# Second-layer tails of a 512-token tile in one row-tiled group over all PSUM banks, with output projections one chunk behind

## The chip, the cores and the metric

The kernel runs on one core of one Trainium2 chip. The metric is the device time of one execution in microseconds (us), as a median over runs. Before the change it is 214.68 us (6 runs, 214.44 to 214.84).

## The reference, cut to what matters

Two branches read the same 2048 x 640 input and a gate mixes them per token. Branch A is a diagonal complex state-space recurrence with an input and an output projection. Branch B is a two-layer perceptron with 1728 hidden features.

```python
x = A_x                                                   # 1 x 2048 x 640
g = sigmoid((x * gate_w).sum(-1, keepdims=True))
# branch A
Bu = einsum("bld,pd->blp", x, B_bar)                      # complex, P = 640
h_t = Lam_bar * h_{t-1} + Bu_t                            # for each token t
a = 2 * einsum("blp,dp->bld", hseq, C).real + x * Dskip
# branch B, F = 1728 = 13 * 128 + 64
hid = gelu(einsum("bsd,df->bsf", x, w1) + b1)
b = einsum("bsf,fd->bsd", hid, w2) + b2
return g * a + (1 - g) * b
```

The 1728 hidden features are 13 full blocks of 128 and a tail of 64. The tail is what the change is about.

## The kernel before

**Tiles.** The 2048 tokens are worked in 4 tiles of 512 (index `q`), in 8 recurrence blocks of 256 (index `b`), and in 16 output chunks of 128 (index `c`, four to a tile). All matmul results go to the 8 PSUM banks, handed out in a ring by `next_bank()`.

**Stages of one tile.**
- `bproj(q)`: input projection of the recurrence, L680, 10 banks of five matmuls. ScalarE moves each bank to `U` (L689).
- `ssm(b)`: VectorE only. Four multiplies and adds ("pre"), two scans (L720) with small carry steps, four multiplies and adds ("post") that write `H[b % 3]`.
- `m1(q)`: first perceptron layer, L640, 13 banks of five matmuls. ScalarE applies the gelu and writes `Gl[q % 2]` (L647).
- `m1_tail(q)`: the 64 tail features of two tiles at once, L658, in one bank. Four gelus on 64 partitions each (L667) write them twice, to partitions 0 to 63 and 64 to 127 of `Gl`.
- `gates(q)`: VectorE row sums, a tanh on ScalarE (L604), and two small VectorE steps that write the gate columns `gcol` and `g1col` (L608, L609).
- `outs(...)`: second layer, output projection and mixing for some chunks.

**Inside `outs`.** For each chunk:
- `m2_prime(c)`: ScalarE writes the bias into the chunk's two banks, one for each half of 320 output columns (L754). The matmuls then add to it.
- `m2_main(c)`: 13 matmuls for each half, 26 in all (L767).
- `m2_tails(cs)`: the 64 tail features for all chunks of the call (L781). The left half uses partitions 0 to 63 and the right half 64 to 127, so two matmuls lie on two row tiles of the array. The group follows the first chunk's main product, so it needs the primed banks of every chunk of the call.
- `m2_out(c)`: ScalarE scales the two banks by `g1col` into `E1[c % 3]` (L795).
- `cproj(c)`: output projection of the recurrence, 10 matmuls for each half (L815), in two further banks. ScalarE scales these by `gcol` into `E2[c % 3]` (L826).
- `comb(c)`: VectorE computes the skip term `xg` (L834), adds `xg`, `E1` and `E2` in two steps (L481, `osb`), and SyncE stores 160 KB (L868). The last chunk adds `xg` and `E1` first, then finishes straight out of PSUM in two column parts of 384 and 256 (L848) with two stores (L854).

**What sets the order.** Each stage registers operations with an engine, an assumed duration, what they read and write, and a priority. A list scheduler (`Sched.order`) then fixes one static order for each engine. An operation of TensorE takes its priority from the order of registration. Each engine runs its list strictly in that order and waits on semaphores for what it needs. `op(..., writes)` makes a writer of a buffer wait for all its earlier readers, so a bank, an `E1` copy or an `H` block is written only after its last use.

## Time and profile before

| quantity | value |
|---|---|
| median of 6 runs | 214.68 us |
| profiled execution, device time | 214.44 us |
| profiled execution, span from first to last instruction | 213.1 us |
| granted TensorE clock | 1.0 of full speed |
| main products, L767 | 416 matmuls, 59.1 us busy |
| tails, L781 | 32 matmuls, 3.4 us busy |
| output projections, L815 | 320 matmuls, 46.1 us busy |
| primes, L754 | 32, 0.441 us each |
| first evictions, L795 | 32, 0.526 us each |
| scans, L720 | 16, 2.812 us each |

The span leaves out 1.34 us of the device time that lies around the instructions. Matmuls are pipelined, so the busy time of a group is not a sum that adds up to the span; the chain of waits in order of time is what shows how long TensorE takes for a stage. Lines of `kernel.py` are written as L and a number. A duration belongs to one profiled execution, and the median of runs is 0.24 us above it.

### The profile page before, as it was taken

How to read it: one execution, taken by the hardware profiler on the slowest of the kernel's cores; microseconds unless marked ns; L12 is line 12 of the kernel's file. 1: busy time of each engine (PE TensorE's matmuls, PEld its weight loads, DVE VectorE, ACT ScalarE, POOL GpSimd, SP SyncE). 2: the span in 40 equal slices, each digit the busy share in tenths (PEclk: the TensorE clock that was granted, in tenths of full speed). 3: DMA queues.
4: the chain of work that ended last, by engine and by line, in shares of the span. 5: the costliest groups of instructions: out<-in, count | busy, mean ns of one | idle time of the engine just before them, and what ended most of it. 6: DMA issues, size and time to landing. Idle time of an engine off the chain costs nothing.

```text
span 213.1 us, 3104 instructions
## 1 busy us (share of the span) xinstructions
PE 209.5 (98%) x1254; PEld 119.8 (56%) x1264; DVE 188.7 (89%) x262; ACT 113.2 (53%) x205; POOL 2.5 (1%) x10
## 2 busy tenths in 40 slices
PE   8999999999999999999999999999999999999996
PEld 3444444444567675444467767444446777677673
DVE  2599999999899999999999959999999998988712
ACT  2489556679444234557835332556786454535230
POOL 1000000000000000000000010000000000000000
PEclk9999999999999999999999999999999999999999
DMA  5999899999000040000000013000000010001000
GB/s 142 332 241 196 222 384 198 159 217 162 0 0 34 31 138 18 31 0 0 0 3 0 31 43 146 22 8 0 3 0 2 0 34 31 31 3 62 31 34 31
DMA packets 31114, 16.08 MB, mean 75 GB/s; under 512 B 22908, under 2 KB 30332, under 8 KB 31100
## 3 DMA queue, kind: packets, MB, share of 16 engines
q1 hardware_dynamic: 30752, 14.57, 28.5%
q0 software_dynamic: 288, 1.31, 1.9%
q8 instruction: 10, 0.16, 0.3%
q14 instruction: 4, 0.03, 0.0%
q10 hardware_dynamic: 60, 0.01, 0.0%
HBM read 7.63 MB, written 2.62 MB: 48 GB/s over the span
## 4 chain that ended last, share of the span: by engine, by line
PE 97%; DMA 1%; issue 0%; DVE 0%
PE ps L767 27%; PE ps L640 22%; PE ps L815 21%; PE ps L680 20%; PE ps L620 4%; DMA xn<-in_A_x_dram 1%; PE ps L781 1%; PE ps L658 1%; PE ps L412 0%; DVE osb L848 0%; PE ps L431 0%
## 5 line engine op out<-in xcount | busy, mean ns | idle before, releaser
L767 PE MATMUL ps<-W2sb,Gl 128*128 128x320 bf16 x416 | 59.1, 299 | 0.0
L767 PEld LDWEIGHTS ps<-W2sb,Gl 128*128 128x128 bf16 x416 | 40.6, 98 | 16.5 <-ACT Gl L647 0.4
L640 PE MATMUL ps<-xT,W1sb 128*128 128x512 bf16 x215 | 47.5, 379 | 0.3
L815 PE MATMUL ps<-CT,H 128*128 128x320 bf16 (+2 forms) x320 | 46.1, 299 | 0.0
L720 DVE TENSOR_TENSOR_SCAN W<-atab,V 128x1280 bf16<-128x1280 f32 x16 | 44.3, 2812 | 0.3
L680 PE MATMUL ps<-xT,BT 128*128 128x512 bf16 x196 | 43.1, 379 | 0.3 <-issue 0.2
L815 PEld LDWEIGHTS ps<-CT,H 128*128 128x128 bf16 x320 | 30.7, 98 | 13.5 <-issue 1.6
L795 ACT ACTIVATE E<-ps,g1col 128x320 bf16<-128x320 f32 x32 | 16.1, 526 | 40.5 <-PE ps L781 21.5
L640 PEld LDWEIGHTS ps<-xT,W1sb 128*128 128x128 bf16 x220 | 21.5, 98 | 26.0
L647 ACT ACTIVATE Gl<-ps,cols 128x512 bf16<-128x512 f32 x44 | 29.7, 690 | 11.6 <-PE ps L640 11.6
L680 PEld LDWEIGHTS ps<-xT,BT 128*128 128x128 bf16 x200 | 19.5, 98 | 23.4 <-ACT Gl L647 0.4
L689 ACT ACTIVATE U<-ps 128x512 bf16<-128x512 f32 x40 | 23.6, 595 | 15.7 <-PE ps L680 15.7
L826 ACT ACTIVATE E<-ps,gcol 128x320 bf16<-128x320 f32 x30 | 15.8, 527 | 18.0 <-PE ps L815 18.0
L754 ACT ACTIVATE ps<-b2b 128x320 f32<-128x320 bf16 x32 | 14.1, 441 | 1.0
L834 DVE SCALAR_TENSOR_TENSOR xg<-xn,gcol,dsk 128x640 bf16<-128x640 bf16 x16 | 13.8, 882 | 0.4
L481 DVE TENSOR_TENSOR osb<-xg,E 128x640 bf16<-128x640 bf16 x15 | 7.3, 486 | 7.7 <-ACT E L826 7.6
L597 DVE SCALAR_TENSOR_TENSOR scr<-xn,gwb 128x640 bf16<-128x640 bf16 x16 | 13.2, 823 | 0.4
L481 DVE TENSOR_TENSOR H<-H,V 128x1280 bf16<-128x1280 bf16 x16 | 12.5, 822 | 0.3
L481 DVE TENSOR_TENSOR V<-V,W 128x1280 bf16<-128x1280 bf16 x16 | 12.5, 821 | 0.3
L481 DVE TENSOR_TENSOR V<-mr,U 128x2560 bf16<-128x2560 bf16 x8 | 11.9, 1490 | 0.2
L481 DVE TENSOR_TENSOR H<-c,W 128x2560 bf16<-128x2560 bf16 x8 | 11.9, 1489 | 0.1
L481 DVE TENSOR_TENSOR V<-s,W 128x2560 bf16<-128x2560 bf16 x8 | 11.9, 1485 | 0.0
(79 smaller groups left out, 102.6 us busy)
## 6 DMA issues: line engine op xcount, KB each, us to landing
out_dram<-osb SPq DMA_DIRECT2D x15, 160.0 KB, 1.8
W2sb<-in_B_w_dram SPq DMA_DIRECT2D x1, 2080.0 KB, 11.1
xn<-in_A_x_dram POOLq DMA_DIRECT2D x2, 640.0 KB, 4.7
W1sb<-in_B_w_dram SPq DMA_DIRECT2D x4, 256.0 KB, 4.3
xn<-in_A_x_dram SPq DMA_DIRECT2D x1, 640.0 KB, 7.2
W1sb<-in_B_w_dram SPq DMA_DIRECT2D x1, 480.0 KB, 5.4
W1sb<-in_B_w_dram SPq DMA_DIRECT2D x1, 400.0 KB, 6.2
xn<-in_A_x_dram SPq DMA_DIRECT2D x1, 384.0 KB, 5.7
```

The source lines that it names most:

```text
L481: return inc("dve", nc.vector.tensor_tensor(out=o, in0=a, in1=b, op=o_))
L640: t = nc.tensor.matmul(PS[bank][:, :], W1sb[:, k, jf * 128:(jf + 1) * 128], xT[q][:, k, :], start=(k == 0), stop=(k == KD - 1))
L647: return inc("act", nc.scalar.activation(Gl[q % 2][:, jf, :], PS[bank][:, :], ACT.Gelu_apprx_tanh, bias=b1col[:, jf:jf + 1]))
L680: t = nc.tensor.matmul(PS[bank][:, :], BT[:, ci, kd, k * 128:(k + 1) * 128], xT[q][:, kd, :], start=(kd == 0), stop=(kd == KD - 1))
L689: return inc("act", nc.scalar.activation(dst, src, ACT.Copy, scale=1.0 if ci == 0 else -1.0))
L720: t = inc("dve", nc.vector.tensor_tensor_scan(out=g[:, ci, :], data0=a, data1=v[:, ci, :], initial=0.0, op0=ALU.mult, op1=ALU.add))
L754: return inc("act", nc.scalar.activation(PS[bank][:, 0:HALF], b2b[:, cols], ACT.Copy))
L767: t = nc.tensor.matmul(PS[bank][:, 0:HALF], Gl[q % 2][:, jf, t4 * 128:(t4 + 1) * 128], W2sb[:, jf, cols], start=False, stop=False, skip_gr ...
L795: return inc("act", nc.scalar.activation(E1[c % NE][:, cols], PS[bank][:, 0:HALF], ACT.Copy, scale=g1col[:, c:c + 1]))
L815: t = nc.tensor.matmul(PS[bank][:, 0:n], H[b % NHB][:, ci, k, s * 128:(s + 1) * 128], CT[:, ci, k, cols], start=(i == 0), stop=(i == 2 * K ...
L826: return inc("act", nc.scalar.activation(E2[c % NE][:, cols], PS[bank][:, 0:HALF], ACT.Copy, scale=gcol[:, c:c + 1]))
L834: return inc("dve", nc.vector.scalar_tensor_tensor(out=xg[c % 2][:, :], in0=xn[q % 2][:, c % 4, :], scalar=gcol[:, c:c + 1], in1=dsk[:, :] ...
```

## The change

Before, a call of `outs` takes two or three chunks, so a tile of four chunks has its tails in two groups (the last two tiles together in three), and a chunk's projection follows its own main product at once. After it, a call takes a whole tile: all eight banks are primed, the first main product runs, and one group of eight tail matmuls serves four chunks. Each chunk's projection and mixing are registered after the next chunk's main product; the last chunk's projection follows that of the chunk before. The recurrence block 7 (`ssm(2 * NQ - 1)`), which stood between two calls, is registered through `mid` within the third tile's call, after the projection of chunk 9. The order of all other stages in the text is as it was. The static orders of ScalarE and VectorE change with it, since the scheduler places their operations by when it expects them to be ready.

```diff
-        def outs(*cs):
+        def outs(q, mid=None):
+            cs = range(4 * q, 4 * q + 4)
             for c in cs:
                 m2_prime(c)
             for c in cs:
                 m2_main(c)
                 if c == cs[0]:
                     m2_tails(cs)
                 m2_out(c)
-                cproj(c)
-                comb(c)
+                if c > cs[0]:
+                    cproj(c - 1)
+                    comb(c - 1)
+                    if mid is not None and c == cs[0] + 2:
+                        mid()
+            cproj(cs[-1])
+            comb(cs[-1])
...
         gates(1)
-        outs(0, 1)
-        outs(2, 3)
+        outs(0)
         for q in range(2, NQ):
...
             gates(q)
             if q < NQ - 1:
-                outs(4 * q - 4, 4 * q - 3)
-                outs(4 * q - 2, 4 * q - 1)
-        outs(NCH - 8, NCH - 7, NCH - 6)
-        ssm(2 * NQ - 1)
-        outs(NCH - 5, NCH - 4, NCH - 3)
-        outs(NCH - 2, NCH - 1)
+                outs(q - 1)
+        outs(NQ - 2, mid=lambda: ssm(2 * NQ - 1))
+        outs(NQ - 1)
```

The new order on TensorE, after `bproj(1)`, reads: 26 main, 8 tails, 39 main (chunk 1 and half of chunk 2), 20 projection, 13 main, 20 projection, 26 main, 40 projection. The later tiles have 26 main, 8 tails, 26 main, 20 projection, 26 main, 20 projection, 26 main, 40 projection. The old order had 26 main, 4 (or 6) tails, 20 projection, and then 26 main and 20 projection in turn.

## The prediction

> **What bounds the kernel now.** I read the page's busy shares first, then its chain of work, then the chain in order of time around one stage, then the tail instructions alone, and last ScalarE's timeline where a prime comes latest.

> ```profile
> PE 209.5 (98%) x1254; PEld 119.8 (56%) x1264; DVE 188.7 (89%) x262; ACT 113.2 (53%) x205; POOL 2.5 (1%) x10
> PE 97%; DMA 1%; issue 0%; DVE 0%
> ```

> TensorE's matmuls fill 98% of the span and carry 97% of the chain that ends last; VectorE is at 89%, ScalarE at 53%. A busy matmul row isn't a proof of pace, so what counts is the chain in time. Its piece for the first two groups of output chunks:

> ```profile
> 56.42 3.53 PE ps L767 x26
> 59.95 0.38 PE ps L781 x4
> 60.33 2.82 PE ps L815 x20
> 63.15 3.53 PE ps L767 x26
> 66.68 2.72 PE ps L815 x20
> 69.40 3.53 PE ps L767 x26
> 72.93 0.38 PE ps L781 x4
> 73.31 2.82 PE ps L815 x20
> 76.13 3.53 PE ps L767 x26
> 79.66 2.72 PE ps L815 x20
> ...
> 182.18 0.51 PE ps L781 x6
> 182.70 2.82 PE ps L815 x20
> ```

> Columns are start, length, what. Each piece begins where the last ends: TensorE waits for nobody here. L767 is a chunk's main product (26 matmuls), L781 the tails, L815 the output projection (20). The reader is to see two things. Four tail matmuls take 0.38 us and six 0.51, so two more, one pair on the two row tiles, cost 0.13. And the projection takes 2.82 after tails but 2.72 elsewhere.

> ```profile
>   issue: 1.8, 7
>   ACT E L795: 21.5, 7
> ```

> These come from the view of line L781: before each of the 7 tail groups weight loading sat idle, 1.8 us together, 0.26 each, with nothing but issue to wait for. The second line says that ScalarE waits for the tails, not the reverse.

> [...] two pairs at 0.13 are 0.26, the group takes 0.38, so 0.12 goes on entry, and 0.10 on the way back, 0.22 per group. [...] here each tail pair needs two banks, hence all eight for four chunks. [...]

> **The change part by part.**

> *Fewer tail groups.* Before there are 7: five of 4 matmuls and two of 6, 5 x (0.38 + 0.10) + 2 x (0.51 + 0.10) = 3.62 us. After there are 4 of 8 matmuls. Eight matmuls weren't seen; by the step from four to six they take 0.51 + 0.13 = 0.64, and 4 x (0.64 + 0.10) = 2.96. Gain 0.66, all on the chain. Bounds: if the two row tiles lost their overlap in a longer group, the added pair would cost 0.26 instead of 0.13, 4 x 0.13 = 0.5 back; it can't be below 0.13, the time of one matmul of the pair (3.53 / 26 = 0.136 for the same 320 columns), so there is no further gain. I take 0.13, because four to six showed it. What follows the tails is now a main product, not a projection; it has the same shape, and 0.12 (0.11 is what it lost after the first-layer tail L658: 3.64 against 3.53) against 0.10 is nothing.

> *The same matmuls otherwise.* The new order on TensorE has the same 416 main, 32 tail and 320 projection matmuls. In the first group the half of the third main product comes ahead of the first projection; order alone costs nothing between full-array matmuls (3.53 and 2.72 follow each other without a gap).

> *Eight primes before the tails.* The group now waits for all eight banks to be written with the bias (L754, 0.44 us each) instead of four. Behind the waiting tail stands all of TensorE. Where the primes stand in ScalarE's queue, by the changed order:
> - First group: a prime follows each U eviction (L689), 0.58 + 0.44 = 1.02 per pair against the 1.08 of a bank's five matmuls (U starts at 54.30, 55.38, 56.46 in ScalarE's timeline). The last eviction starts at 56.46, so the last prime ends near 57.5; the tails start at 59.95. Slack 2.4.
> - Second: gelu and prime pairs. They keep the pace of 1.08 in the trace, see below. The last gelu starts at 107.24, the last prime ends near 108.4, the tails start at 110.73. Slack 2.3.
> - Third, the tight one: the eighth prime takes the bank of the first-layer tail (L658), so it stands behind four 64-partition gelus (L667).

> ```profile
> 156.58 0.44 ACT L754 ACTIVATE ps<-b2b 128x320 f32<-128x320 bf16 x1
> 156.96 0.67 ACT L647 ACTIVATE Gl<-ps,cols 128x512 bf16<-128x512 f32 x1
> 157.66 0.44 ACT L754 ACTIVATE ps<-b2b 128x320 f32<-128x320 bf16 x1
> 158.04 0.67 ACT L647 ACTIVATE Gl<-ps,cols 128x512 bf16<-128x512 f32 x1
> 159.23 2.81 ACT L667 ACTIVATE Gl<-ps,cols 64x512 bf16<-64x512 f32 x4 [0.52 <-PE ps L658]
> 162.75 0.58 PE L781 MATMUL ps<-W2sb,Gl 64*128 64x320 bf16 x6
> ```

> The reader is to see that gelu and prime overlap a little, so that a pair fits into 1.08, and that 0.52 of idle time after the last gelu takes a seventh prime (0.44). The four tail gelus end at 162.04, the eighth prime at 162.48, and the tails are due at 162.8: slack 0.3. Before, they needed only two of those gelus. Bounds for a stall: 0 to 0.2, [...] I take 0.
> - Fourth: primes follow projection evictions, the last one about 1.1 us after the last projection of the third group; the tails are 3.5 after it. Slack 2.4.

> *Projections one chunk behind.* Each chunk's projection uses banks that the first eviction (L795, 0.53) cleared a main product earlier, so the bank wait is looser. In the first group VectorE now runs the scan (5.54, with its small steps 6.3) before it computes the gate columns. So the first eviction can start only near 56.67 + 6.3 + 0.3 = 63.3 instead of 60.37. Its banks are wanted at the first projection, which starts after tails, one and a half main products: 60.59 + 0.10 + 3.53 + 1.77 = 66.0. Slack 2.

> *Buffers.* E1 has three copies and is now filled one main product plus one projection, 6.3 us, ahead. The eviction of chunk 7 (L795) waits for the sum of chunk 4, which in VectorE's order moved behind a scan: counted from the second group's start, that sum ends at 16.2 (pre-work ends 8.9, scan 6.3, sum 1.0) and is wanted at 18.5. If late it would hold ScalarE, then chunk 7's projection at 23.0. The H blocks are read later than before and their writers wait: block 3 (written from 106.42) needs the projection of chunk 1, over by 73.2; block 7 is placed after chunk 9's projection. The input load of tile 2 on GpSimd's queue waits for chunk 3's VectorE product, some 4 us later than 74.1; its data are first read after 132. SyncE's queue has the same stores in the same order.

> *The end.* The projection of chunk 14 now comes after the last main product, so its eviction and its sum (L481, two of 0.49) stand just before the last chunk's finishing steps. Before, that sum ended 1.61 us after chunk 14's projection and the first finishing step began 1.67 after the last projection's start. So it fits with 0.06 to spare, and the second step has another 0.47 of idle time. The 160 KB store of chunk 14 is issued about 1.6 us ahead of the last one; such stores land in 1.8. I take 0 for it; bounds below.

> **Sum.** Profiled execution: span 213.10 plus 1.34 around it = 214.44. Minus 0.66: 213.78. The median shown is 0.24 above the profiled run, so 214.68 - 0.66 = 214.0.

> **Rivals.** "Same" below is within 0.2%, 0.43 us, about what this measurement can tell from no change.
> - *Gain eaten by small waits*: the third group's 0.3 slack fails by 0.2 and the end store adds some 0.2, or longer groups pack worse (up to 0.5 back). Speaking for it: the slack is thin and a group of eight wasn't seen. Against: gelu and prime kept pace six times in a row. 0.66 - 0.4 leaves 0.26: 214.4. Chance 0.19.
> - *The end store decides, slower*: the last store queues behind chunk 14's 160 KB. If the last three stores were strictly one after another, with 1.8, 1.6 and 1.5 us, the last would land 1.8 later. It turns the gain into a loss beyond 0.2% from 0.66 + 0.43 = 1.09 on. Against: before, the last two stores overlapped by 0.65 us and each still landed in 1.6 and 1.5. At the full price: 214.0 + 1.8 = 215.8; at 1.3, which I'd expect of it, 215.3. Chance 0.11.
> - *The change doesn't do what it says*: excluded by the instruction order, which shows four groups of eight.

> **How the numbers follow.** The forecast (214.0) has 0.70. Its own range is 213.7 to 214.25: 0.3 below for the scatter of the medians (runs shown span 0.40) and up to where 0.2% ends. The second case reaches to 214.6, and the range 213.7 to 214.6 leaves out the slower case and a little of the rest. Faster 0.70, same 0.19, slower 0.11.

> **What would show it.** In the changed profile: L781 pieces of x8 at 0.64, main products of 3.63 after them, every projection of 2.72; a TensorE chain of the same unbroken form, span near 212.4. I'd be wrong if L781 is preceded by a wait for L754 (third group first), if L815 waits for L795, or if the stretch from the last matmul to the end of the span, 2.1 us before, grows.

## The result, and the profile after

The median fell from 214.64 us (42 runs, among them the 6 with 214.68 above) to 214.13 us (21 runs, 213.64 to 214.61). The ratio is 0.9975 with a 95% interval of 0.9968 to 0.9982, so between 0.39 and 0.69 us were gained. The profiled execution took 213.86 us, with a span of 212.5.

The page's busy shares and chain of work, after:

```profile
PE 208.3 (98%) x1254; PEld 119.9 (56%) x1264; DVE 189.1 (89%) x262; ACT 113.4 (53%) x205; POOL 2.5 (1%) x10
PE 95%; DMA 2%; issue 1%; ACTq 1%; POOL 0%; DVE 0%; POOLq 0%
```

TensorE still carries the chain. The 2% of DMA are a load at the very start (the bias rows, 4.51 us from 2.61 on), not a wait in the stages that changed. The chain in order of time (start, length, what), first tile and third tile:

```profile
56.47 3.53 PE ps L767 x26
60.01 0.65 PE ps L781 x8
60.66 5.40 PE ps L767 x39
66.06 2.72 PE ps L815 x20
68.78 1.77 PE ps L767 x13
70.54 2.72 PE ps L815 x20
73.26 3.53 PE ps L767 x26
76.79 5.43 PE ps L815 x40
...
158.81 3.64 PE ps L767 x26
162.45 0.65 PE ps L781 x8
163.10 3.64 PE ps L767 x26
166.74 2.72 PE ps L815 x20
...
204.99 5.45 PE ps L815 x40
```

Three things are to be seen. The pieces still join without a gap (a single record of L767 lasts 0.299 us in both profiles and 26 of them take 3.53, so records overlap and only the pieces are compared). A group of eight takes 0.65 us. And the extra 0.10 to 0.11 now falls on the main product after the tails (3.64 against 3.53; 5.40 for 39 against 1.5 x 3.53 = 5.30), while a projection of 20 takes 2.72 everywhere. The 3.64 at 158.81 stands ahead of the tails: it follows the first-layer tail (L658), as it did before the change.

The last projection of the kernel before is this piece of its chain:

```profile
208.28 2.73 PE ps L815 x20
```

From the start of the first main product to the end of the last matmul TensorE needed 208.28 + 2.73 - 56.42 = 154.59 us before and 204.99 + 5.45 - 56.47 = 153.97 after, so 0.62 less. This measure, called the *stretch* below, leaves out the start of the kernel, in which TensorE has the same work in all kernels here but which ended anywhere between 56.31 and 56.94 in their profiles. That scatter is as large as the gain, and it passes on to the whole: the two profiled runs of the changed kernel (213.86 and, in the next section, 214.21) differ by 0.35 us, and the starts of their first main products by 0.36. So the medians need many runs to show the gain.

### The profile page after: what moved, and what is told of

It is laid out like the page before. It is cut to its first block, busy times and chain, and to the rows that moved or that the text cites. A ratio compares the mean times of both kernels' runs of the same rounds, so it can differ in the third digit from the quotient of the medians.

```text
span 212.5 us, 3107 instructions
## 1 busy us (share of the span) xinstructions
PE 208.3 (98%) x1254; PEld 119.9 (56%) x1264; DVE 189.1 (89%) x262; ACT 113.4 (53%) x205; POOL 2.5 (1%) x10
## 4 chain that ended last, share of the span: by engine, by line
PE 95%; DMA 2%; issue 1%; ACTq 1%; POOL 0%; DVE 0%; POOLq 0%
PE ps L767 27%; PE ps L640 22%; PE ps L815 20%; PE ps L680 20%; PE ps L620 3%; DMA rows<-in_B_b_dram 2%; PE ps L781 1%; PE ps L658 1%; ACTq L325 1%; DVE osb L848 0%; POOL io_i L381 0%; PE ps L431 0%; POOL rows L371 0%; POOL st_i L383 0%; POOL st_i L382 0%
## 5 line engine op out<-in xcount | busy, mean ns | idle before, releaser
L767 PE MATMUL ps<-W2sb,Gl 128*128 128x320 bf16 x416 | 59.2, 299 | 0.0
L767 PEld LDWEIGHTS ps<-W2sb,Gl 128*128 128x128 bf16 x416 | 40.3, 98 | 17.2 <-issue 1.1
L815 PE MATMUL ps<-CT,H 128*128 128x320 bf16 (+2 forms) x320 | 45.4, 299 | 0.0
L815 PEld LDWEIGHTS ps<-CT,H 128*128 128x128 bf16 x320 | 31.3, 98 | 12.2
L795 ACT ACTIVATE E<-ps,g1col 128x320 bf16<-128x320 f32 x32 | 16.2, 526 | 37.8 <-PE ps L767 25.0
L640 PEld LDWEIGHTS ps<-xT,W1sb 128*128 128x128 bf16 x220 | 21.5, 98 | 26.0
L647 ACT ACTIVATE Gl<-ps,cols 128x512 bf16<-128x512 f32 x44 | 29.6, 688 | 10.4 <-PE ps L640 10.4
L689 ACT ACTIVATE U<-ps 128x512 bf16<-128x512 f32 x40 | 23.6, 595 | 14.4 <-PE ps L680 14.4
L481 DVE TENSOR_TENSOR osb<-xg,E 128x640 bf16<-128x640 bf16 x15 | 7.3, 487 | 9.2 <-ACT E L826 9.2
L754 ACT ACTIVATE ps<-b2b 128x320 f32<-128x320 bf16 x32 | 14.1, 442 | 1.1
L481 DVE TENSOR_TENSOR H<-H,V 128x1280 bf16<-128x1280 bf16 x16 | 12.5, 822 | 0.3
L481 DVE TENSOR_TENSOR V<-V,W 128x1280 bf16<-128x1280 bf16 x16 | 12.5, 821 | 0.3
L481 DVE TENSOR_TENSOR V<-mr,U 128x2560 bf16<-128x2560 bf16 x8 | 11.9, 1490 | 0.3
L481 DVE TENSOR_TENSOR H<-c,W 128x2560 bf16<-128x2560 bf16 x8 | 11.9, 1488 | 0.1
L481 DVE TENSOR_TENSOR W<-mi,U 128x2560 bf16<-128x2560 bf16 x8 | 11.9, 1485 | 0.0
```

The source lines that it names most:

```text
L481: return inc("dve", nc.vector.tensor_tensor(out=o, in0=a, in1=b, op=o_))
L640: t = nc.tensor.matmul(PS[bank][:, :], W1sb[:, k, jf * 128:(jf + 1) * 128], xT[q][:, k, :], start=(k == 0), stop=(k == KD - 1))
L647: return inc("act", nc.scalar.activation(Gl[q % 2][:, jf, :], PS[bank][:, :], ACT.Gelu_apprx_tanh, bias=b1col[:, jf:jf + 1]))
L689: return inc("act", nc.scalar.activation(dst, src, ACT.Copy, scale=1.0 if ci == 0 else -1.0))
L754: return inc("act", nc.scalar.activation(PS[bank][:, 0:HALF], b2b[:, cols], ACT.Copy))
L767: t = nc.tensor.matmul(PS[bank][:, 0:HALF], Gl[q % 2][:, jf, t4 * 128:(t4 + 1) * 128], W2sb[:, jf, cols], start=False, stop=False, skip_gr ...
```

## The experiments

Each kernel is the changed one with one edit, and "after" is the changed kernel. "Stretch" is read from its own chain in the same way.

**The changed kernel again** (no edit), for a comparison beside the next three.

> The changed kernel as it is, beside the others. Both theories: 0.9975 of before, within 0.9968 to 0.9982; some 214.1 us.

Measured: 214.11 us, ratio 0.9971 (0.9959 to 0.9982), stretch 153.96. The result repeats.

**Two groups of four for each tile.**

```diff
-                if c == cs[0]:
-                    m2_tails(cs)
+                if c % 2 == 0:
+                    m2_tails((c, c + 1))
```

> Projections one chunk behind as after, but two groups of four tails per tile, 8 groups in all. If each group costs a fixed 0.22 us for entering and leaving the row tiles: 4 groups more than after, +0.88, 215.0 us, and 0.22 above before with its 7. If the later projections bring the gain and not the number of groups: as after, 214.1 us.

Measured: 214.95 us, ratio 1.0004 (0.9995 to 1.0013), stretch 154.81, between these two pieces of its chain:

```profile
56.46 3.53 PE ps L767 x26
...
205.82 5.45 PE ps L815 x40
```

That is 0.84 more than after, or 0.21 for each of four added groups, and 0.22 more than before for one added group. The projections are one chunk behind as after, and yet nothing is left of the gain. So the number of groups makes the gain, not the place of the projections.

**One group of two for each chunk.**

```diff
-                if c == cs[0]:
-                    m2_tails(cs)
+                m2_tails((c,))
```

> As after, but each chunk has its own group of two tails, 16 groups. Fixed price per group: 12 more than after, 12 x 0.22 = +2.64, 216.8 us, with L781 pieces of x2 at 0.25 us. If the number of groups doesn't matter: 214.1 us.

Measured: 216.66 us, ratio 1.0093 (1.0079 to 1.0108), stretch 156.51: 2.54 more than after, again 0.21 for each of twelve groups. Its chain, and what stood ahead of its tails in the view of line L781:

```profile
56.39 3.53 PE ps L767 x26
...
207.10 0.24 PE ps L781 x2
207.35 5.55 PE ps L815 x40
...
  issue: 4.0, 15
```

A group of two takes 0.24 and costs 0.10 on the 40 projection matmuls behind it (5.55 against the 5.45 of the same last piece after the change). Weight loading sat idle 0.27 us ahead of each of 15 groups with nothing but issue to wait for, about as it did before. With 0.24, 0.38, 0.51 and 0.65 for two, four, six and eight tails, a pair costs 0.135 and the entry into the group 0.11.

**Projections registered at once.**

```diff
-                if c > cs[0]:
-                    cproj(c - 1)
-                    comb(c - 1)
-                    if mid is not None and c == cs[0] + 2:
-                        mid()
-            cproj(cs[-1])
-            comb(cs[-1])
+                cproj(c)
+                comb(c)
+                if mid is not None and c == cs[0] + 1:
+                    mid()
```

> Four groups of eight as after, but each projection is registered right after its own main product; the scheduler puts half a main product between where it expects a wait. If the number of groups makes the gain: as after, 214.1 us, no wait on TensorE. If being one chunk behind makes it: as before, 214.6 us.

Measured: 214.24 us, ratio 0.9974 (0.9963 to 0.9985), stretch 153.96, and no wait of TensorE in the tiles. The list scheduler put main products between the tails and the first projection by itself: one and a half in the first tile, half a one in each of the other three. First and second tile:

```profile
61.00 5.40 PE ps L767 x39
66.41 5.43 PE ps L815 x40
...
111.57 1.87 PE ps L767 x13
113.44 2.72 PE ps L815 x20
```

So being a whole chunk behind isn't needed in the last three tiles; half a main product to run while the first eviction is done is enough. The first tile, where the eviction waits for the scan, had its cover here too.

**Projections forced to be at once.** The same edit, and each main product is held until the projection before it is done, so the scheduler can't put anything between.

```diff
-                   [("bank", bank)], f_mm, prio=pe_prio())
+                   [("bank", bank)], f_mm, prio=pe_prio(), after=last_c)
...
-                op(f"c_{c}_{hf}", "pe", ...)
+                last_c[:] = [op(f"c_{c}_{hf}", "pe", ...)]
```

> Four groups of eight, and each main product is held until the projection of the chunk before is done, so the first projection of a tile follows the tails at once. If being behind covers the wait for the first eviction: in the first tile the projection waits for the gate columns after the scan, 63.3 + 0.53 - 60.7 = 3.1 us, in the other three for one eviction, 0.58 each; 4.8 in all, 218.9 us. If the order has no part in it: 214.1 us.

Measured: 221.25 us, ratio 1.0305 (1.0287 to 1.0324). The waits of TensorE, and the first projection of the first tile and a later one in the chain (the lines have moved by one: L816 is the projection, L796 the first eviction):

```profile
PE ps L816 <- ACT E L796: 5.2, 4, 3.3
...
64.33 4.26 PE ps L816 x20
72.12 2.72 PE ps L816 x20
```

The waits are there, 5.2 us in four places with 3.3 the longest, against 4.8 with 3.1 expected. Another 1.5 us is no wait: the 20 matmuls after the longest one took 4.26 instead of 2.72. The view by windows shows why. Its columns are the window, its length, busy time of PE, PEld, DVE, ACT and POOL (with instructions), the granted clock, and DMA.

```profile
56.00:60.50 4.50, 4.50 (x34) 2.91 (x34) 4.43 (x5) 1.98 (x5) 0.00 (x0) 1.00 0.00 0
60.50:64.20 3.70, 0.51 (x8) 0.13 (x4) 3.60 (x8) 0.54 (x2) 0.00 (x0) 0.94 0.00 0
64.20:66.00 1.80, 1.67 (x7) 1.01 (x8) 1.80 (x3) 0.40 (x1) 0.00 (x0) 0.50 0.00 0
66.00:68.50 2.50, 2.50 (x16) 1.59 (x15) 2.46 (x3) 0.53 (x1) 0.00 (x0) 0.77 0.00 0
68.50:72.00 3.50, 3.50 (x28) 2.51 (x27) 3.43 (x6) 1.05 (x2) 0.00 (x0) 1.00 0.15 51
```

The clock granted to TensorE was 0.50 right after the wait and full again from 68.5 on at the latest. If it stood in the mixed windows at either the 0.50 or the 1.00 of the others, the 0.94 and the 0.77 put the half speed between about 63.8 and 67.15, some 3.4 us (an estimate from these windows; 3.4 us at 0.50 in a span of 219.7 also make a mean of 0.992, which is what this run shows). The matmuls that start at 64.33 then lose some 1.4 us by it (an estimate: half of 2.8 us), nearly all of the 1.5.

**Tails over the full array.** The second 64 rows of the tail weights are zero and each tail runs over all 128 rows, so the tiling mode doesn't change for the tails: the profile names their tile 128*128, as that of the main products, where it was 64*128. The sums are the same.

```diff
-        load("w2c", "sp", "l_w2c", W2sb[64:64 + FL, NF - 1, :], ...)
+        def f_w2z():
+            return inc("dve", nc.vector.memset(W2sb[64:64 + FL, NF - 1, :], 0.0))
+        op("w2z", "dve", 0.6, (), ["w2c"], f_w2z, prio=-50)
...
-                        r = slice(64 * hf, 64 * hf + FL)
+                        r = slice(0, 128)
```

> Four groups of eight tails over all 128 rows, with zeros in the second 64 rows of the weights, so no change of tiling mode. Each tail then takes a full 0.136 us: 32 x 0.136 = 4.35 against 4 x 0.75 = 3.0. If the fixed 0.22 per group is the change of mode: +1.35, 215.5 us, and the pieces before and after the tails at their plain lengths. If any group costs it, its semaphore wait for one: another 0.88, 216.4 us.

Measured: 215.65 us, ratio 1.0041 (1.0025 to 1.0057), stretch 155.29, 1.32 more than after. Its chain in the second tile (L785 are the tails here, L771 the main products):

```profile
107.75 3.53 PE ps L771 x26
111.28 1.09 PE ps L785 x8
112.36 3.53 PE ps L771 x26
```

Eight tails take 8 x 0.136 = 1.09 with nothing on entry, and the main product behind them its plain 3.53. Weight loading no longer sat idle ahead of these tails. The group still waits for the same banks and still signals once at its end. So the fixed 0.21 belongs to the change of tiling mode, not to a group as such.

**Tails ahead of the first main product**, so that a late eighth prime shows as a wait.

```diff
+                if c == cs[0]:
+                    m2_tails(cs)
                 m2_main(c)
-                if c == cs[0]:
-                    m2_tails(cs)
```

> The group of eight before the first main product, so that nothing covers the wait for the eighth prime. By the placement of the primes on ScalarE the tails wait 1.1 us in the first tile, 1.2 in the second, 3.3 in the third (behind the four tail gelus), 1.1 in the fourth: 6.7 together, 220.9 us. If the primes were ready much earlier: under 216 us.

Measured: 222.96 us (221.38 to 224.59), ratio 1.0410 (1.0376 to 1.0445); the profiled execution took 221.38. Its waits of TensorE in the tiles:

```profile
PE ps L781 <- ACT ps L754: 5.7, 3, 3.4
PE ps L781 <- ACT gth L604: 1.3, 1, 1.3
```

Together 7.0 us against 6.7 expected, and the longest, 3.4, stands in the third tile behind the tail gelus. The second line is the first tile, where the wait is put down to the tanh that follows the eighth prime on ScalarE. So the eighth prime comes where the placing on ScalarE's queue had put it. The other runs of this kernel were 1.5 to 3.2 us longer than the profiled one, at a mean granted clock of 0.992 and 0.985 instead of 1.0.

**Chunk 14's projection back before the last main product**, all else as after.

```diff
-                if c > cs[0]:
+                if c > cs[0] and c < NCH - 1:
...
+                if c == NCH - 2:
+                    cproj(c)
+                    comb(c)
```

> As after, but chunk 14's projection is put before the last main product, as it stood before the change, so that its sum and its store are out of the way at the end. If the end costs nothing: as after, 214.1 us. If the store of chunk 14 or its sum takes back the missing 0.13 us: 214.0 us and a shorter stretch after the last matmul.

Measured: 214.18 us, ratio 0.9976 (0.9966 to 0.9986), stretch 153.96. From the end of the last matmul to the end of the span there are 2.1 us, as in the changed kernel (212.5 - 210.44). The late store and sum of chunk 14 cost nothing.

**Tails by halves:** first the four left halves, then the four right ones.

```diff
-                for c in cs:
-                    q, t4 = c // 4, c % 4
-                    for hf in range(2):
+                for hf in range(2):
+                    for c in cs:
+                        q, t4 = c // 4, c % 4
```

> As after, but in each group the four left halves come first and then the four right ones, so neighbours in the queue share a row tile. If a pair costs 0.13 because its two matmuls run side by side on two row tiles: nearly every matmul now takes 0.13 alone, a group goes from 0.65 to about 1.2 (8 x 0.13 + 0.12), four of them +2.1, 216.2 us. If a tail of 64 rows is simply half as long, whatever its neighbour: 214.1 us.

Measured: 214.29 us, ratio 0.9976 (0.9968 to 0.9984), stretch 154.01, and groups of 0.66. The expected loss is missing. Either a 64-row matmul is short whatever lies beside it, or a right half starts before left halves that stand ahead of it. The next run tells them apart.

**All eight tails on one row tile.**

```diff
-                        r = slice(64 * hf, 64 * hf + FL)
+                        r = slice(0, FL)
```

> As after, but all eight tails of a group take the features from partitions 0 to 63, so all lie on one row tile. If the 0.13 per pair is two row tiles at work side by side (and the tails by half were short because a right half could still start beside a left one): each matmul takes 0.13 alone, a group goes from 0.65 to about 1.2, +2.1 over four groups, 216.2 us. If a 64-row matmul is as short on one row tile: 214.2 us, and the second copy of the tail features isn't needed.

Measured: 216.38 us, ratio 1.0077 (1.0055 to 1.0098), stretch 156.13, 2.16 more than after. A group took 1.19 (third tile; compare 0.65):

```profile
159.74 3.64 PE ps L767 x26
163.37 1.19 PE ps L781 x8
164.56 3.64 PE ps L767 x26
```

So one row tile alone needs 0.135 for each matmul, and the pair is short only because two row tiles work at once. It follows for the kernel by halves that right halves ran beside left ones although they stand four places behind. Its timeline agrees, though it doesn't say which half a tail belongs to. The view of a short window shows the matmuls under way in it; this one lies 0.16 to 0.19 us after the first tail, and the one below it 0.22 to 0.27 us after the first tail of the kernel on one row tile. By halves:

```profile
60.41 0.46 PE L781 MATMUL ps<-W2sb,Gl 64*128 64x320 bf16 x4
```

One row tile:

```profile
59.78 0.44 PE L781 MATMUL ps<-W2sb,Gl 64*128 64x320 bf16 x2
```

Within 0.19 us four tails have begun in the one, and within 0.27 us only two in the other. So the four can't all be left halves.

No version beat the changed kernel. The one with the projections at once, the one with chunk 14's at once and the one by halves lie within its interval.

## Why the prediction was right

The forecast was 214.0 us, a gain of 0.66; measured were 0.51 between the medians, with an interval that holds 0.66, and 0.62 on TensorE's stretch.

- *Fixed price of a group, 0.22.* Right, and 0.21 by the three counts of groups (7, 8 and 16 against 4). Three groups at that difference are the 0.04 between 0.66 and 0.62. The rest of the way to 0.51 is within the scatter of medians: the same kernel, run again beside its own reference, had 0.70 between them (214.81 and 214.11). That the price belongs to the change of tiling mode was the author's reading and not shown by the profile before; the run with full-array tails shows it, with 1.09 for eight tails of 0.136 and the plain 3.53 behind them. Neither the end nor the third tile gave anything back: putting chunk 14's projection at once moved nothing, and the stretch has no wait in it.
- *Eight tails at 0.64.* They took 0.65 in all four groups. The prediction's bound on the other side, 0.5, lets only the added pair of each group lose its overlap. A group whose four pairs all lose it is what the kernel on one row tile has, and that cost 2.16, four times as much. So the bound was too narrow for the case in which the row tiles don't overlap at all; that case didn't come.
- *Eight primes.* No tail waited. In the third tile, the tightest, the four gelus, the eighth prime and the tails stood as placed:

```profile
158.86 2.81 ACT L667 ACTIVATE Gl<-ps,cols 64x512 bf16<-64x512 f32 x4
161.69 0.44 ACT L754 ACTIVATE ps<-b2b 128x320 f32<-128x320 bf16 x1
162.38 0.39 PEld L781 LDWEIGHTS ps<-W2sb,Gl 64*128 64x128 bf16 x8 [0.26 <-ACT ps L754]
```

  The prime ended at 162.13, the tails began with the end of the main product at 162.45: slack 0.3. The bound of 0.2 for a stall was the author's estimate; where the prime does end last, in the third tile of the kernel with the tails first, the tails began 0.05 us behind it (165.22 against 164.72 + 0.45). The 0.26 put down to L754 is the same 0.26 of idle weight loading that stands ahead of every group, and the chain has no gap there.
- *Gate columns behind the scan.* The first eviction started at 63.31 (63.3 predicted) and the first projection at 66.06 (66.0), so ScalarE's wait of 5.6 us for the gate columns cost TensorE nothing. The run with forced projections shows what that wait is worth without the cover.
- *Sum of chunk 4.* It ended at 122.41, 15.4 us after its tile's start (16.2 predicted), 3 us before the eviction that needs its buffer.
- *The end.* The sum of chunk 14 ended at 209.32 and the first finishing step began at 209.37.

```profile
208.83 0.49 DVE L481 TENSOR_TENSOR osb<-osb,E 128x640 bf16<-128x640 bf16 x1
209.37 0.62 DVE L848 SCALAR_TENSOR_TENSOR osb<-ps,gcol,E 128x384 bf16<-128x384 f32 x1
210.46 0.48 DVE L848 SCALAR_TENSOR_TENSOR osb<-ps,gcol,E 128x256 bf16<-128x256 f32 x1 [0.47 <-PE ps L815]
```

  The slower rival, three stores one after another, didn't come: the last two landed in 1.6 and 1.5 us as before.
- *What was said wrongly.* The sentence above that each engine runs its list strictly in order doesn't hold between row tiles: in the kernel by halves right halves ran beside left ones four places ahead of them, and a group took 0.66 against 1.19 on one row tile. The forecast didn't rest on it beyond the claim that all of TensorE stands behind a waiting tail. The kernel with the tails first bears that out for full-array products: in its third tile TensorE stood still for 3.4 us, the tails began at 165.22 and the main products behind them at 165.94.

## What to carry to other kernels

Where an engine's chain has no gaps, count what it pays for each switch of mode (0.21 us for a group here) and make the switches fewer; such a price is visible in the pieces around the switch (0.38 for two pairs of 0.135, and 0.10 on the piece behind), where medians need many runs to show it. A wider group needs all its buffers at once, so place the last of them on the queue that fills it, and compare with the work that covers it. A distance from a fixed start to a fixed end within the profile repeated to 0.01 us (153.96 and 153.97 in the four kernels of the same length) where medians scattered by 0.1 (214.11 to 214.24).
